# Output gates by tanh, the gates of chunks 1 to 5 on 80 rows, and a new early order

## The chip, the core and the metric

One core of a Trainium2 chip runs the whole program once. The metric is device time in microseconds of one execution; before the change it is 418.37 us (median of 3 runs, 418.22 to 418.58).

## The reference, cut

Three layers follow each other, all in float32: a gated linear attention (an mLSTM) over 2 batches, 8 heads, 768 steps of 40 features, a product of two projections, and a layer with the Mish function.

```python
for t in range(S):                       # attention, per batch and head
    m_new = np.maximum(f_gate[:, :, t] + m, i_gate[:, :, t])
    f_stab = np.exp(f_gate[:, :, t] + m - m_new)
    i_stab = np.exp(i_gate[:, :, t] - m_new)
    C = f_stab * C + i_stab * outer(v_t, k_t);  n = f_stab * n + i_stab * k_t
    o = 1.0 / (1.0 + np.exp(-o_gate[:, :, t]))
    y[:, :, t] = o * (C @ q_t) / np.maximum(np.abs(n @ q_t), 1.0)
h = ((x @ w1) * (x @ w2)) @ w3           # 1536 x 320 -> 1024
x = h @ w_out
h = x @ w_in                             # 320 -> 2048
out = (h * tanh(softplus(h))) @ w_out2
```

## The kernel before, in words

**Tiling.** The 768 steps are 6 chunks of 128; a unit is one chunk of one batch with its 8 heads, so there are 12 units, u = 2 * chunk + batch. Two chunks of both batches are a block of 512 tokens, and the two later layers run block by block (3 blocks). A unit is a chain over the engines: `E` (TensorE, exponents of the decay), `dw` (ScalarE, exp), `vw` (GpSimd, weighted values), `S` (TensorE, q times k), `wg` (VectorE, S times weights), `Y` (TensorE), `I` (TensorE, the state's part), `U` and `st` (state update), `cb` (VectorE, sum of both parts), `r1` to `r3` (denominator), `xs` and `xo` (output gate and denominator), `dup`, `X` (transposes), `Xe` and `Xl` (high and low half of the result for the next layer). The state of one batch passes from unit u to u + 2. `A`, `B` are the products with w1 and w2, `W` is w3 times w_out, `X1` the product with that, `H` and `O` the last layer. Weights come as pieces (load, `mag`, `clamp`, `bits1` to `bits`, `hi`, `lo`): float64 bits turned into two float32r parts, mostly on VectorE.

**Gates.** `start()` prepares the decays. f and i lie on all 128 partitions as 8 copies of the 16 rows (batch, head). Chunk 0 goes first, then the stages chunk 1 and chunks 2 to 5: running maximum `pa` (L879), two tensor_tensor `pt`, `pb` (L895), prefix sum `pc` (L900), then splits into high and low parts `lr`, `ll`, `less`, `la0`, `la1`, `lb0`, `lb1`; `te` transposes the sums on TensorE and `turn` takes their exponent. `rb` and `rc` spread a chunk's sums over the heads (ex_r).

**Order.** Each step is a node with an engine, a due time (table DUE), a duration, and dependencies. `Work.plan` places the nodes by these and so fixes the order of every engine's instructions. Where it sees TensorE idle it puts in products nobody reads, `keep_warm` (L594, tile psz), which keep TensorE's clock up; their number is fixed in the program. Engines wait for each other by semaphores when it runs, each in its own fixed order.

**Output gate.** `add_sigmoids` (L814) applies Sigmoid to 2 and then 4 tiles, on ScalarE; `xs` multiplies by it on GpSimd. The sigmoid needs another function table than exp.

Of the kernel before, what the change touches and what calls it, by code (L numbers as in the profile page):

```python
# [10 lines left out]
F32 = mybir.dt.float32  # L11
# [15 lines left out]
    sgg=(2, 4), mu=8, s_pe=0.268, s_act=0.543, s_dve=0.435, s_pool=0.206, ahead=1, w0n=5, ff=0.972, gd=0.0,  # L27
    ph=0.071, a0=-12.81, ap=-93.853, a_ld=-1652.39, e_e=8363.2, e_s=3345.95, e_r=2252.59, g_ld=6316.58,
# [3 lines left out]
    c_o2=88.35, cp_o2=12.531, c_wi=-5894.32, c_o3=-2264.6, m0=232.0, grp=8, mp0=-162.897, mp=204.465, m_o=1263.83,  # L32
# [3 lines left out]
    mag_w12='ACT', mag_wo='ACT', mag_w3='ACT', mag_wi='DVE', mag_o2='DVE', mag_o3='DVE', lo_w12='DVE', lo_wo='DVE',  # L36
    lo_w3='POOL', lo_wi='POOL', lo_o2='DVE', lo_o3='DVE', xo='POOL', vw='POOL', dup='ACT', rb0='DVE', rc0='DVE',
    rb1='DVE', rc1='DVE', rb='ACT', rc='ACT', st0='DVE', cb0='DVE', prep='ACT', g_tt='DVE', g_ll='DVE',
    lo_w120='DVE', lo_w121='DVE', lo_w122='DVE', lo_w123='DVE', lo_w124='DVE', lo_w125='POOL', lo_w126='DVE',
    lo_w127='POOL',  # L40
# [4 lines left out]
    set_0=0.0, ld_o_0=0.6, ld_g=1.3, ld_qk_0=1.7, ld_kv_0=1.8, load_0=1.9, ld_o_1=4.6, lr_0=4.8, less_0=2.3,  # L45
    ll_0=4.5, la1_0=5.1, la0_0=5.4, rb_0=5.6, one_0=5.7, lb0_0=40.7, lb1_0=6.2, pl_1=6.1, rc_0=6.4, pl_0=18.6,
    E_0=5.8, pa_1=7.7, pr_1=15.4, pa_2=7.8, E_1=7.5, dw_0=8.0, ld_qk_1=8.7, pt_1=9.7, S_0=9.2, pt_2=9.4,
    ld_kv_1=23.2, pb_1=10.6, dw_1=7.0, pb_2=11.3, pc_1=11.4, pc_2=11.7, te_1=16.7, lr_1=11.5, turn_1=7.0,
    less_1=13.1, te_2=11.7, lr_2=24.7, less_2=13.8, load_1=14.8, turn_2=13.5, ll_2=13.9, la1_2=13.7, ll_1=14.5,
    sgm_0=14.3, ld_o_2=24.2, vw_0=4.4, lb1_2=13.6, U_0=-11.7, ld_qk_2=16.0, rb_1=11.7, wg_0=16.2, la0_2=16.4,  # L50
    sgm_1=17.3, vw_1=16.8, ld_kv_2=16.6, la1_1=16.9, st_0=17.9, Y_0=-10.7, la0_1=13.8, mag_0=16.9, lb0_2=18.8,
    lb0_1=19.0, set_1=19.1, lb1_1=-2.1, rc_1=19.4, S_1=19.3, clamp_0=20.0, rb_2=20.1, cb_0=20.6, load_2=18.4,
    E_2=18.1, wg_1=21.0, xs_0=23.9, r1_0=19.4, mag_1=20.5, E_3=22.0, ld_o_3=20.4, r2_0=17.9, bits1_0=11.3,
    dw_2=20.6, U_1=22.5, r3_0=27.8, bits2_0=25.1, Y_1=22.8, ld_qk_3=23.3, st_1=23.8, xo_0=31.7, bits_0=26.7,
    ld_kv_3=26.0, dw_3=23.6, S_2=24.4, cb_1=24.0, vw_2=24.7, r1_1=24.3, I_2=-2.3, rc_2=25.2, wg_2=26.2, U_2=27.2,
    xs_1=31.5, dx_2=25.6, dup_0=23.1, Ie_2=29.8, hi_0=26.6, E_4=28.1, load_3=16.7, st_2=38.2, Y_2=28.6, dw_4=29.5,
# [1290 lines left out]
```

## Time and profile before

| what | value |
|---|---|
| median of 3 runs | 418.37 us |
| the profiled execution, its time | 418.2 us |
| its span | 416.5 us |
| TensorE (PE) busy | 409.5 us, 98% |
| VectorE (DVE) busy | 291.1 us, 70% |
| ScalarE (ACT) busy | 197.7 us, 47% |
| GpSimd (POOL) busy | 80.4 us, 19% |

A row of a timeline gives start, duration, engine, line, operation, output<-inputs, shape and how many were merged. The duration of merged products includes the last one's drain, so the price of a block is the distance from its start to the start of the next one. Times are from the start of the span.

### The profile page before, as it was taken

The numbers are of one execution on the slowest core, as the hardware profiler recorded it, in microseconds if no ns is written. First come the engines' busy times: TensorE is split into PE (matmuls) and PEld (weight loads), VectorE is DVE, ScalarE is ACT, GpSimd is POOL, SyncE is SP. The second block draws the span as 40 slices with busy tenths as digits, with TensorE's granted clock in tenths as the row PEclk, the third lists the DMA queues.
The fourth block names the chain that finished last, engine by engine and source line by source line (L and its number), as shares of the span: only waits on it lengthen the run. The fifth ranks groups of instructions, "written<-read, shape, count | busy, mean of one in ns | idle before, by whom it ended". The sixth has DMA issues, their size and how long they took to land.

```text
span 416.5 us, 7129 instructions
## 1 busy us (share of the span) xinstructions
PE 409.5 (98%) x2815; PEld 359.8 (86%) x2815; DVE 291.1 (70%) x527; ACT 197.7 (47%) x381; POOL 80.4 (19%) x78
## 2 busy tenths in 40 slices
PE   8999999999999999999999999999999999999996
PEld 5689988798888899988888888989989999889995
DVE  7999999999899969779999987789231041330221
ACT  8787967444544444542644376157051161340430
POOL 3234264345102242431001132300000000000000
PEclk9999999999999999999999999999999999999999
DMA  7957744433313543445243253420100000100002
GB/s 238 324 178 220 239 119 153 139 97 127 114 50 102 168 136 101 150 139 166 65 104 87 64 127 90 164 63 2 65 0 2 0 2 2 63 2 0 2 2 64
DMA packets 30497, 40.88 MB, mean 98 GB/s; under 512 B 1856, under 2 KB 24640, under 8 KB 30464
## 3 DMA queue, kind: packets, MB, share of 16 engines
q1 hardware_dynamic: 29952, 39.95, 31.4%
q8 instruction: 22, 0.36, 0.4%
q10 hardware_dynamic: 512, 0.48, 0.4%
q14 instruction: 11, 0.09, 0.1%
HBM read 38.45 MB, written 1.97 MB: 97 GB/s over the span
## 4 chain that ended last, share of the span: by engine, by line
PE 93%; DVE 5%; DMA 1%; ACT 0%; issue 0%; DVEq 0%
PE pso L1210 21%; PE psh L1186 20%; PE psb L1057 11%; PE psa L1057 10%; PE psw L1028 7%; PE psY L699 5%; PE psS L650 3%; PE psx L1097 3%; PE psx L1099 3%; PE psx L1098 3%; PE psI L661 2%; PE psx L1102 1%; PE psx L1101 1%; PE psE L624 1%; DVE gates L410 1%; PE psX L743 1%
## 5 line engine op out<-in xcount | busy, mean ns | idle before, releaser
L410 DVE TENSOR_TENSOR gl<-u,gh 128x512 fp32r<-128x512 f32 x48 | 32.9, 691 | 68.7 <-ACT u L1195 68.7
L1191 ACT ACTIVATE gh<-psh 128x512 fp32r<-128x512 f32 x48 | 28.8, 601 | 79.5 <-PE psh L1186 79.4
L1186 PE MATMUL psh<-xd,wih 64*128 64x512 f32 x240 | 59.4, 395 | 0.0
L1186 PEld LDWEIGHTS psh<-xd,wih 64*128 64x128 f32 x240 | 43.1, 184 | 3.6 <-ACT u L1195 0.2
L1210 PE MATMUL pso<-wo,gh 128*128 128x320 f32 x192 | 42.6, 310 | 0.0
L1186 PE MATMUL psh<-hs,wih 64*128 64x512 f32 x144 | 41.6, 395 | 0.0
L502 DVE SCALAR_TENSOR_TENSOR f<-raw,f 128x640 int32<-128x640 int32 (+2 forms) x44 | 40.0, 908 | 0.9
L507 DVE SCALAR_TENSOR_TENSOR f<-raw,f 128x640 int32<-128x640 int32 (+2 forms) x44 | 37.7, 858 | 0.9
L410 POOL TENSOR_TENSOR th<-f,th 128x512 fp32r<-128x512 f32 x16 | 22.1, 1381 | 62.1 <-ACT th L512 59.1
L1210 PEld LDWEIGHTS pso<-wo,gh 128*128 128x128 f32 x192 | 32.0, 188 | 1.1 <-issue 1.1
L1186 PE MATMUL psh<-xd,wil 64*128 64x512 f32 x120 | 31.6, 391 | 0.0
L1186 PE MATMUL psh<-hs,wil 64*128 64x512 f32 x120 | 31.4, 391 | 0.0
L1210 PE MATMUL pso<-wo2h,gh 128*128 128x320 f32 x96 | 30.0, 312 | 0.0
L1210 PE MATMUL pso<-wo2h,gl 128*128 128x320 f32 x96 | 29.6, 309 | 0.0
L1210 PE MATMUL pso<-wo2l,gh 128*128 128x320 f32 x96 | 29.6, 309 | 0.0
L1210 PE MATMUL pso<-wo,gl 128*128 128x320 f32 x96 | 29.6, 309 | 0.0
L1057 PE MATMUL psa<-hs,w12h 128*128 128x512 f32 x72 | 28.9, 401 | 0.1
L1195 ACT ACTIVATE u<-psh 128x512 f32<-128x512 f32 x48 | 28.9, 603 | 0.0
L1057 PE MATMUL psb<-hs,w12h 128*128 128x512 f32 x72 | 28.3, 394 | 0.2 <-DVE y L410 0.2
L1186 PEld LDWEIGHTS psh<-hs,wih 64*128 64x128 f32 x144 | 25.7, 184 | 3.2 <-issue 1.3
L1028 PE MATMUL psw<-woh,th 128*128 128x320 f32 x128 | 28.5, 310 | 0.0
L493 DVE TENSOR_SCALAR f<-f 128x640 f32<-128x640 f32 (+2 forms) x44 | 23.6, 536 | 7.0 <-ACT f L487 6.3
(146 smaller groups left out, 1031.8 us busy)
## 6 DMA issues: line engine op xcount, KB each, us to landing
raw<-in_w_dram SPq DMA_DIRECT2D x16, 512.0 KB
raw<-in_w_out_dram SPq DMA_DIRECT2D x12, 640.0 KB
raw<-in_w_dram SPq DMA_DIRECT2D x16, 384.0 KB
raw<-in_w_in_dram SPq DMA_DIRECT2D x16, 320.0 KB
kv<-in_kv_dram SPq DMA_DIRECT2D x12, 324.0 KB
qk<-in_qk_dram SPq DMA_DIRECT2D x24, 160.0 KB
sg<-in_o_gate_dram SPq DMA_DIRECT2D x12, 160.0 KB
out_dram<-yo SPq DMA_DIRECT2D x9, 160.0 KB
```

The source lines that it names most:

```text
L410: return eng.tensor_tensor(out=o, in0=a, in1=b, op=op)
L493: nc.vector.tensor_scalar(out=ff, in0=ff, scalar1=HI_MIN, scalar2=HI_MAX, op0=ALU.max, op1=ALU.min)
L502: nc.vector.scalar_tensor_tensor(out=f, in0=t["raw"][:, :, 1], scalar=-0x40000000, in1=f, op0=ALU.bitwise_and, op1=ALU.bitwise_or)
L507: nc.vector.scalar_tensor_tensor(out=f, in0=t["raw"][:, :, 0], scalar=29, in1=f, op0=ALU.logical_shift_right, op1=ALU.bitwise_or)
L650: nc.tensor.matmul(t["S"][g][:, p * T:(p + 1) * T], lhsT=t["qk"][rows, 1, p, :], rhs=t["qk"][rows, 0, p, :], start=True, stop=True)
L699: nc.tensor.matmul(ps[:, h * VW:(h + 1) * VW], lhsT=t["w"][:, h, :], rhs=t["v"][:, h, :], start=True, stop=True)
L1028: nc.tensor.matmul(ps, lhsT=t[a][:, 0, c * 128:(c + 1) * 128], rhs=wo[b], start=(c0 + c + s == 0), stop=(c0 + c == KC - 1 and s == 2))
L1057: nc.tensor.matmul(ps, lhsT=a, rhs=b, start=(n == 0 and not begun), stop=(n == len(seq) - 1))
L1186: nc.tensor.matmul(mt[i + k]["ps"], lhsT=w[k][:, c], rhs=x[k][c], start=(n == 0 and c == 0), stop=(n == 2 and c == KC2 - 1))
L1191: nc.scalar.activation(out=t["gh"], in_=t["ps"], func=AF.Mish)
L1195: nc.scalar.activation(out=t["u"], in_=t["ps"], func=AF.Mish)
L1210: nc.tensor.matmul(ps, lhsT=t[a][:, sl], rhs=wo[b], start=(ft == 0 and n == 0), stop=(ft == KF2 - 1 and n == 2))
```

## The change

1. The output gates use Tanh at half the argument, so that sigmoid is (tanh + 1) / 2; `xs` becomes one scalar_tensor_tensor (plus 1, times y) on VectorE, and `r2` doubles the denominator. One gate tile per instruction, 6 times.
2. The gates of chunks 1 to 5 are computed on 80 rows (5 chunks x 16) of 128 columns: one running maximum of 16 rows x 640 (`pa`), five products that put the maxima on the 80 rows (`mv`), one pass of `pt`, `pc`, `less`, a split (`lr`, `ll`, `la`, `lb`), ten products that spread them back over 128 partitions (`rp`), and nine copies out of PSUM (`evL`, `ev0`, `ev1`). `prep_sel` builds the selection matrices on GpSimd. The gate loads shrink from 2 x 128 x 640 to 2 x 16 x 640 plus 2 x 80 x 128.
3. The decay of the state, `sd`, is a node of its own, on GpSimd for units 2, 3, 5, 6, 7 and 9, on VectorE for 4 and 8.
4. The causal mask by TensorE is for 7 units instead of 8 (`mu`); unit 7 gets it from GpSimd (`ms`).
5. New due times for the first hundred microseconds, `keep_warm` at the start 7 instead of 5, rules that prefer the same form of product, and a guard that adds `keep_warm` products. The last layer may use more buffers in the last block.

```diff
-    sgg=(2, 4), mu=8, ... ahead=1, w0n=5, ff=0.972, gd=0.0,
+    sgg=(1, 1, 1, 1, 1, 1), mu=7, ... ahead=1, w0n=7, ff=1.0,
+    gd=0.316, ph=1.362, ...
...
-    la0_0=5.4, ...
+    ... sd_8=67.5, sd_6=75.5, evL_0=15.3, rp_1=-0.1, ps_0=35.2, ...
...
-            if c > 0:
-                s = st[b].rearrange("a p (e v) -> a (p e) v", e=2)
-                tt(nc.vector, s, s, t["d"].unsqueeze(2).to_broadcast([128, H, VW]), mult)
+        def sd():
+            s = st[b].rearrange("a p (e v) -> a (p e) v", e=2)
+            tt(nc.gpsimd if sd_e == "POOL" else nc.vector, s, s, t["d"].unsqueeze(2).to_broadcast([128, H, VW]), mult)
...
-            nc.vector.tensor_scalar_max(out=t["r"], in0=t["r"], scalar1=1.0)
+            (nc.gpsimd if r2_e == "POOL" else nc.vector).tensor_scalar(out=t["r"], in0=t["r"], scalar1=1.0, scalar2=2.0,
+                                                                        op0=ALU.max, op1=mult)
...
-            tt(nc.gpsimd if ENG["xo"] == "POOL" else nc.vector, xh, t["y"][:, :, 0:D], sg[kb, b][:, j % 2], mult)
+            nc.vector.scalar_tensor_tensor(out=xh, in0=sg[kb, b][:, j % 2], scalar=1.0, in1=t["y"][:, :, 0:D], op0=add, op1=mult)
...
-                nc.scalar.activation(out=o, in_=o, func=AF.Sigmoid)
+                nc.scalar.activation(out=o, in_=o, func=AF.Tanh, scale=0.5)
...
+        def ld_c():
+            for o, a in ((f1, f_gate), (i1, i_gate)):
+                nc.sync.dma_start(out=o, in_=a[0:G, F:S])
+            for o, a in ((cf, f_gate), (ci, i_gate)):
+                nc.sync.dma_start(out=o, in_=by_chunk(a[0:G, F:S]))
+        def mv():
+            gps["m"] = bank("psg")
+            for c in range(NK):
+                a = F + c * T
+                nc.tensor.matmul(gps["m"][0:NC, 0:T], lhsT=sel_m[:, NC - G - c * G:2 * NC - G - c * G], rhs=m[0:G, a:a + T],
+                                 start=(c == 0), stop=(c == NK - 1))
+        def rp(n):
...
+                for e in range(2):
+                    a = 32 + c % 2 * G - 32 * e
+                    nc.tensor.matmul(o, lhsT=sel_r[r, a:a + 128], rhs=chi[r, 2 * e * T:2 * (e + 1) * T], start=(e == 0), stop=(e == 1))
+        add_node(("pa", 1), "DVE", due, scan(S1), lambda: nc.vector.tensor_tensor_scan(
+            out=m[0:G, F + 1:S + 1], data0=f1, data1=i1, initial=m[0:G, F:F + 1], op0=add, op1=ALU.max), [("ld_c",)], port=True)
+        add_node(("mv", 1), "PE", due, 1.1, mv, [("pa", 1), ("ps", 0)], [(AT, [("pt", 1)])], warm=0.3)
```

**ScalarE, the first microseconds.** Names: ex_l and ex_r are the operands of `E`, sel_b and sel_h constants for them; CAST gates 64x128 is `lr` of chunk 0. Before:

```order
L871 CAST causal<-z 128x512
L857 CAST ex_l_88<-sel_b 64x128
L857 CAST ex_l_89<-sel_b 64x128
L905 CAST gates<-gates 64x128
L931 ACTIVATE ex_l_89<-gates,neg_b 64x128
L931 ACTIVATE ex_l_88<-gates,neg_b 64x128
L867 ACTIVATE ones_92<-ident 64x128
```

and with the change:

```order
L919 CAST causal<-z 128x512
L895 CAST ex_l_88<-sel_b 64x128
L895 CAST ex_l_89<-sel_b 64x128
L895 CAST ex_l_88<-sel_b 64x640
L895 CAST ex_l_89<-sel_b 64x640
L1032 CAST gates<-gates 64x128
L905 ACTIVATE ones_92<-ident 64x128
L905 ACTIVATE ones_93<-ident 64x128
L1016 ACTIVATE ex_l_88<-gates,neg_b 64x128
```

The two copies of 640 columns now stand ahead of `lr` of chunk 0; before they came after it.

**VectorE, from `ll` of chunk 0 to the first `wg`** (w<-psS). Before:

```order
L410 TENSOR_TENSOR gates<-gates 32x128
L410 TENSOR_TENSOR ex_r_90<-gates,sel_h 64x512
L935 SCALAR_TENSOR_TENSOR ex_l_89<-gates,neg_b,ex_l_89 32x128
...
L879 SCALAR_TENSOR_TENSOR gates<-gates 128x512
L410 TENSOR_TENSOR gates<-gates 128x512 x2
L410 TENSOR_TENSOR gates<-gates 128x128 x2
...
L900 SCALAR_TENSOR_TENSOR gates<-gates 128x128 x5
...
L935 SCALAR_TENSOR_TENSOR ex_l_89<-gates,neg_b,ex_l_89 32x512
L410 TENSOR_TENSOR w<-psS,w 128x4x128 x2
```

and with the change:

```order
L418 TENSOR_TENSOR gates<-gates 32x128
L1047 SCALAR_TENSOR_TENSOR gates<-gates 16x640
L1019 SCALAR_TENSOR_TENSOR ex_l_89<-gates,neg_b,ex_l_89 32x128
L418 TENSOR_TENSOR ex_r_90<-gates,sel_h 64x512
...
L418 TENSOR_TENSOR gates<-gates,psg 80x128
L418 TENSOR_TENSOR gates<-gates 80x128
L935 TENSOR_SCALAR gates<-gates 80x128
L936 SCALAR_TENSOR_TENSOR gates<-gates 80x128
L940 SCALAR_TENSOR_TENSOR gates<-gates 80x128
L418 TENSOR_TENSOR split<-gates,split 80x128
L418 TENSOR_TENSOR w<-psS,w 128x4x128 x2
```

The running maximum of all later chunks moved ahead of the operands of the first `E`, and six short instructions take the place of the long ones.

**TensorE, from the first products to the second `Y`.** psz is `keep_warm`, psg the gates (`mv`, `te`, `rp`). Before, from the end of the first four `E` pairs:

```order
L650 MATMUL psS<-qk_78 128x128 x8
L594 MATMUL psz<-causal,identr 128x512 x5
L675 MATMUL psU<-vw,kv 40x41 x8
L594 MATMUL psz<-causal,identr 128x512 x2
L943 MATMUL psg<-ident,gates 128x16
...
L943 MATMUL psg<-ident,gates 128x16 x4
L594 MATMUL psz<-causal,identr 128x512 x10
L699 MATMUL psY<-kv,w 128x41 x8
L623 MATMUL psE<-causal,identr 128x512
```

and with the change, from the same place, which now has `te` (psg<-ident) between the `E` of unit 0 and that of unit 1:

```order
L1024 MATMUL psg<-ident,gates 128x80
...
L663 MATMUL psS<-qk_78 128x128 x8
L688 MATMUL psU<-vw,kv 40x41 x8
L606 MATMUL psz<-causal,identr 128x512 x4
L715 MATMUL psY<-kv,w 128x41 x8
L975 MATMUL psg<-split,sel 128x256 x10
L663 MATMUL psS<-qk_79 128x128 x8
L688 MATMUL psU<-vw,kv 40x41 x8
L606 MATMUL psz<-causal,identr 128x512 x6
L715 MATMUL psY<-kv,w 128x41 x8
L606 MATMUL psz<-causal,identr 128x512 x2
L674 MATMUL psI<-st_80,qk_78 128x82 x4
```

The `E` of units 2 and 3, which came right after the first `Y` and ahead of the second, now come after both; `keep_warm` products are 21, 1, 4, 6 and 2 up to there, against 12, 5, 2, 2 and 10.

## Rows read from the trace of the kernel before

**Rows 1.** Busy time by stretch: us, busy us and count of each engine, granted clock, DMA.

```profile
0.00:10.00 10.00, 8.14 (x22) 5.57 (x24) 7.84 (x21) 8.12 (x16) 3.88 (x14) 1.00 0.77 231
...
350.00:400.00 50.00, 50.00 (x387) 45.46 (x386) 12.17 (x19) 16.25 (x32) 0.00 (x0) 1.00 0.04 14
```

**Rows 2.** The keep_warm line: count, duration ns min/median/max, first and last start.

```profile
L594 PE MATMUL psz<-causal,identr x33: 388/396/796, 4.4 to 36.8; 128*128 128x512 f32 x33
```

**Rows 3.** Timeline of TensorE, first products: start us, us, what.

```profile
4.37 3.35 PE L594 MATMUL psz<-causal,identr 128*128 128x512 f32 x7 [0.35 <-ACT causal L871]
...
15.53 2.56 PE L594 MATMUL psz<-causal,identr 128*128 128x512 f32 x10 [0.31 <-ACT eT L947]
17.94 2.18 PE L699 MATMUL psY<-kv,w 128*128 128x41 f32 x16
```

**Rows 4.** Timeline of TensorE, 25 to 38 us.

```profile
25.59 1.10 PE L661 MATMUL psI<-st,qk 128*128 128x82 f32 x8
...
26.66 1.16 PE L650 MATMUL psS<-qk 40*128 40x128 f32 x16
27.76 0.51 PE L675 MATMUL psU<-vw,kv 128*40 128x41 f32 x16
28.19 0.98 PE L594 MATMUL psz<-causal,identr 128*128 128x512 f32 x3
29.01 0.39 PE L623 MATMUL psE<-causal,identr 128*128 128x512 f32 x1
...
29.94 1.87 PE L699 MATMUL psY<-kv,w 128*128 128x41 f32 x16
31.64 0.48 PE L623 MATMUL psE<-causal,identr 128*128 128x512 f32 x1
...
36.00 1.17 PE L594 MATMUL psz<-causal,identr 128*128 128x512 f32 x4
37.01 1.88 PE L699 MATMUL psY<-kv,w 128*128 128x41 f32 x16
```

**Rows 5.** Timeline of VectorE, 5 to 18 us: gates and the first wg.

```profile
5.35 0.29 DVE L410 TENSOR_TENSOR gates<-gates 32x128 fp32r<-32x128 f32 x1
5.67 0.69 DVE L410 TENSOR_TENSOR ex_r<-gates,sel_h 64x512 fp32r<-64x512 f32 x1
6.37 0.34 DVE L935 SCALAR_TENSOR_TENSOR ex_l<-gates,neg_b,ex_l 32x128 fp32r<-32x128 f32 x1
...
7.87 1.81 DVE L879 TENSOR_TENSOR_SCAN gates<-gates 128x128 f32<-128x128 f32 x2
9.71 2.50 DVE L410 TENSOR_TENSOR gates<-gates 128x512 f32<-128x512 f32 x4
...
17.02 1.29 DVE L410 TENSOR_TENSOR w<-psS,w 128x512 f32<-128x512 f32 x2
```

**Rows 6.** Timeline of VectorE, 18 to 26 us: work between the first and second wg.

```profile
18.22 0.66 DVE L692 COPY st<-psU 40x164 f32<-40x164 f32 x2
...
22.13 0.50 DVE L711 COPY y<-psY 128x328 f32<-128x328 f32 x1
...
23.94 0.55 DVE L493 TENSOR_SCALAR f<-f 128x768 f32<-128x768 f32 x1
...
25.69 0.96 DVE L502 SCALAR_TENSOR_TENSOR f<-raw,f 128x768 int32<-128x768 int32 x1
```

**Rows 7.** Timeline of ScalarE, 5 to 18 us.

```profile
5.02 0.29 ACT L905 CAST gates<-gates 64x128 fp32r<-64x128 f32 x1 [0.19 <-DVE gates L900]
...
6.44 0.72 ACT L857 CAST ex_l<-sel_b 64x640 fp32r<-64x640 f32 x1
...
16.40 1.28 ACT L814 ACT_TABLE_LOAD   x1
```

**Rows 8.** Groups by form, 0 to 110 us (VectorE) and the whole span (GpSimd).

```profile
L410 DVE TENSOR_TENSOR st<-st,d 128x328 f32<-128x328 f32 x8 | 4.4, 548 | 0.3 <-ACT d L639 0.3
...
L410 POOL TENSOR_TENSOR vw<-kv,w 128x328 f32<-128x328 f32 x10 | 9.9, 992 | 20.4 <-DMA kv<-in_kv_dram 17.8 <-DMA qk<-in_qk_dram 2.6
```

More of the change, by code (lines that the diff above doesn't have):

```diff
@@ L322, in plan @@
             if e == "PE" and self.form[n] != form:
[L323 removed]
+                last += TUNE["sw"]
                 form = self.form[n]
@@ L330, in plan @@
                 port = free[e]
-            if size:
+            if size < 0:
+                end[n] = free[e] - size
+            if size > 0:
                 dma = max(dma, s + 1.6) + max(0.45, size / 243e3)
@@ new lines, in gate_sum, with less, cut @@
+        def gate_sum(f, i, L, skip=0):
+            nc.vector.tensor_scalar(out=f, in0=i, scalar1=0.0, scalar2=-120.0, op0=ALU.min, op1=ALU.max)
+            nc.vector.tensor_tensor_scan(out=L[:, skip:], data0=one[0:L.shape[0], skip:], data1=f[:, skip:], initial=0.0,
+                                         op0=mult, op1=add)
+        def less(i, L):
+            nc.vector.scalar_tensor_tensor(out=i, in0=i, scalar=0.0, in1=L, op0=ALU.max, op1=add)
+        def cut(a, c):
+            return a[:, c * T:(c + 1) * T]
@@ new lines, in start @@
+        for b in range(B):
+            add_node((f"la{b}", 0), "ACT", due, act(T) + 0.1, lambda b=b: la(b), [("less", 0)])
+            add_node((f"lb{b}", 0), "DVE", due, dve(T), lambda b=b: lb(b), [(f"la{b}", 0)], port=True)
+        due = K["g1"]
+        for b in range(B):
+            add_node(("pl", b), ENG["prep"], due - 2, act(640) if ENG["prep"] == "ACT" else 0.75,
+                     lambda b=b: prep_l(b, T, S, ENG["prep"]))
+        add_node(("pr", 1), ENG["prep"], due - 1, act(1024) if ENG["prep"] == "ACT" else 1.2,
+                 lambda: prep_r(1, ENG["prep"]))
@@ new lines, in start @@
+        add_node(("pc", 1), "DVE", due, dve2(T) + scan(T), lambda: gate_sum(cf, ci, cL), [("pt", 1)], port=True)
+        add_node(("less", 1), "DVE", due + 1, dve(T), lambda: less(ci, cL), [("pc", 1)], port=True)
+        for k, (nm, nl, a, x) in enumerate((("lr", "ll", cL, "pc"), ("la", "lb", ci, "less"))):
+            h, l = chi[:, k * T:(k + 1) * T], chi[:, (2 + k) * T:(3 + k) * T]
+            add_node((nm, 1), "ACT", due, act(T), lambda h=h, a=a: nc.scalar.copy(h, a), [(x, 1)])
+            add_node((nl, 1), "DVE", due, dve(T), lambda h=h, l=l, a=a: tt(nc.vector, l, a, h.bitcast(F32), sub), [(nm, 1)], port=True)
@@ L1154, with group @@
     MH = places("b", 4)
-    GP, UP, YP = places("z", 16), places("z", 4, 16), places("z", 6, 25)
+    UP = places("z", 4, 16)
+    def group(i):
+        return next((a, b) for a, b in zip(K["grp"], K["grp"][1:]) if a <= i < b)
     acc = {}
```

407 lines of the change are left out of this document (220 added, 187 removed).

## The prediction

> **What bounds the kernel now.** I read the busy times by stretch first. In the last stretch TensorE is busy 50.00 of 50.00 us while VectorE has 45.46 [rows 1]; in the first ten microseconds it is busy 8.14 us at a mean granted clock of 0.77. So late on only the amount of TensorE's work counts, and at the start a chain over other engines does. Over the whole run TensorE is busy 98% of the span. Some of that is filler: the keep_warm line has 33 rows [rows 2], the first at 4.4 and the last at 36.8 us. So the question for any saving on VectorE, ScalarE or GpSimd is whether it lets TensorE begin its real work earlier, and the question for any saving on TensorE is how many real products go.
>
> Then I read TensorE's timeline. The first seven fillers take 3.35 us, nearly half a microsecond each, which is the lower clock level; the ten from 15.53 to the start of Y at 17.94 take 2.41 us, 0.24 each, the upper one [rows 3]. Before 17.94 TensorE waits for the gates. From there on it is packed, but for two fillings: three keep_warm products from 28.19 to 29.01 (0.82 us) and four from 36.00 to 37.01 (1.01 us) [rows 4]. Prices are taken from one start to the next in the same rows: I 1.07, S 1.10, U 0.43, E of a unit 0.93, Y 1.70.
>
> What the packed part waits for at its start is VectorE's chain. After the three operands of unit 0 (0.69, 0.34 and their like) come the scans of the later chunks (1.81 us from 7.87), four 128x512 passes (2.50 us) and the rest of the gates, until the first wg at 17.02 [rows 5]: 9.15 us in which no wg could run. That is the place where the change could earn something.
>
> **The change part by part.** The comparison is made at one point, the start of S of unit 2, since by then both orders have done the same products: E of units 0 to 3, S, U and Y of 0 and 1, I of 2. Before, that is at 26.66 us [rows 4].
>
> *The start.* ScalarE's copy of unit 0's gate now stands behind two 640-column copies of 0.72 us each; it ran at 5.02 for 0.29 us [rows 7], and I put it at about 6.1 to 6.4. VectorE's ll then ends near 6.75. The one scan of 16x640 has as many columns as the two scans that took 1.81 us [rows 5], with one start less: 1.6 us, to 8.35. Unit 0's four operands (two of 0.34, two of 0.69, and gaps) go to 10.45. Before, all that was over at 7.87, so unit 0's E is some 2.6 us later. E ends about 10.9. Four instructions on 80x128 follow; the nearest rows are the 0.29 and 0.34 of 32x128 [rows 5], and with gaps they take 1.45 us, to 11.9. If they cost as much as the widest of the short ones, 0.55 for 128x768 [rows 6], that would be 0.9 more; below, I allow a tenth off the whole chain. The transpose of the sums waits for them, and TensorE with it, about 1.0 us. Then E of unit 1 from 12.1, S of unit 0 until 14.2, wg of unit 0 from 14.4 to 15.7 (1.29 [rows 5]). This wg started at 17.02 before: the shorter gates win 2.6 us here, though the operands came later. Y of unit 0 would end at 17.4, where before it started at 17.94 and ended 1.70 later, near 19.65.
>
> *Between the first and second wg.* The ten spreading products have half a filler's columns, so half its 0.24: 1.2 us together. S and U of unit 1 follow, to 20.2, then six fillers (1.45), to 21.6. VectorE has meanwhile st 0.66, the second xs in its new form about 0.50 (the 128x328 copy is the nearest row), cb 0.50 and one 128x768 bits pass 0.96 [rows 6]; two state decays of 0.55, from the eight that took 4.4 us [rows 8]; one operand of 0.69 [rows 5]; small and PSUM copies of 0.29 and 0.42 (between 0.29 for 128 and 0.69 for 512 columns). Their sum is 5.6; I take 5.4, as one of them may slip behind. So the second wg runs from 21.1 to 22.4, and TensorE has waited 0.8 us. Y of unit 1 to 24.1, two fillers 0.5, I 1.07, E of units 2 and 3 1.9: S of unit 2 starts at 27.6. **The term is +0.95 us.** The 2.3 us by which the first Y ended earlier are spent on the ten products, more fillers, and a second wg that is not brought forward as much as the first.
>
> For the lower end: with no wait from 11.9 on, te 0.2, the products and fillers named sum to 14.6, and S of unit 2 starts at 26.7, the term is nil. For the upper end, the short instructions at 0.55: +1.85.
>
> *After that.* Both orders have seven more fillers. In before they took 0.82 + 1.01 = 1.83 us [rows 4]; in the change they stand as 1, 1, 2, 2 and 1, 7 x 0.24 = 1.7. **-0.15 us.** They are written into the program and take their time whether a wait is there or not.
>
> *The causal mask* for seven units instead of eight takes away two products of the filler's shape, 2 x 0.24 [rows 3]: **-0.48 us**, since TensorE is packed there. GpSimd does it instead, in about 1.5 us.
>
> *Tanh.* It shares a table with the exponent, so the order has two loads left of six, 4 x 1.28 us [rows 7] less on ScalarE. I cost it at nothing: ScalarE is busy 47% of the span, and in the packed part TensorE waits for it only where the fillers stand, which stay. The xs on VectorE adds about 12 x 0.5, what the gates save there is about as much, and six state decays of 0.55 leave [rows 8]. Nothing on TensorE's path is late by it before the last block, and there 4.5 us of 50 are free [rows 1].
>
> *The gate loads* shrink by 0.49 MB, 2 us at the 231 GB/s of the first stretch [rows 1]. I book nothing, because the first chain waits for unit 0's gate and ScalarE, not for these; kv comes earlier by it, which helps GpSimd.
>
> *The sum.* 0.95 - 0.15 - 0.48 = +0.3 us on the profiled execution of 418.2 us: 418.5. The median lies 0.17 above that execution, so **418.7 us** against 418.37. A measurement can tell some 0.2% here, 0.84 us; this is no measurable change, with bounds of the early term from 417.75 to 419.6.
>
> **The rivals.** *The early chain is shorter than booked (faster).* The chain on VectorE runs from 6.75 to 22.4. If the 80-row instructions and the PSUM copies cost a tenth less in all (1.5 us of 15.7), TensorE's waits of 1.0 and 0.8 us mostly go, and the time is 1.4 less: 417.3. For it: half of that chain has only one nearest row, and fewer partitions move less. Against it: a 64x512 operand at 0.69 us is no quicker per column than the 128x512 passes, 2.50 for four [rows 5], so rows don't matter, columns do, and those I have counted.
>
> *The state decay on GpSimd stands in a queue (slower).* The decay took 0.55 us on VectorE and would take 0.99 on GpSimd by the vw of the same shape; those ten vw have 20.4 us of idle time ahead of them, 17.8 of it for kv by DMA [rows 8]. GpSimd works in its order: a decay placed behind a vw whose kv hasn't landed waits for that load, and the state, I and Y of unit u + 2 behind it. For unit 5 the order has it behind the vw of units 4 and 5. If kv lands 1.6 us after the decay is ready, its extra 0.44 and this make 2.0 us in a packed TensorE: 420.7. It decides from the point where kv of unit 5 lands after the decay's exponent. Against it: the 17.8 us are a sum of ten, mostly GpSimd early at a load, and the gate loads leave DMA freer.
>
> *The clock (slower).* The two fresh gaps near 11 and 21.6 us could drop the granted clock to its lower level. Before, TensorE also waited ahead of 15.53, and the ten fillers behind ran at 0.24 us [rows 3], the upper level, so a gap of that size cost nothing. If it does here, E, S and U behind the gap (2.46 us) run at half rate, and with what follows that is +2.0: 420.7. The Trainium skill ("TensorE: Matmul & The Clock Gate", "HAM oscillation — how this bites in real kernels") says that idle gaps between bursts throttle the engine again and each next burst starts cold, which speaks against an order that waits ahead of te; by it the sum would be 420.7. The trace so far goes the other way.
>
> *Tanh brings table loads of its own (slower).* Then ScalarE has some six loads more than the order shows, two of them at 1.28 us ahead of an exponent that is waited for: 421.3. The order has one load ahead of the Mish table, so I hold this unlikely.
>
> **How the numbers follow.** The forecast has 0.46, of which 0.06 lies above +0.2%, by the upper bound of the early term. The shorter chain has 0.31, the queue 0.14, the clock 0.06, the tables 0.03. So faster 0.31, same 0.40, slower 0.29. The forecast's own range is 417.8 to 419.6. The whole one goes down to 416.8, half a microsecond beyond the shorter chain's time, leaving out perhaps a third of that case (0.10), and up to 421.0, which takes in the queue and the clock with some left over (0.08 out).
>
> **What would show it.** In the changed profile's TensorE timeline: unit 0's E done near 10.9 us, a gap of about 1.0 ahead of te, the first Y from 15.7, the second from 22.4, S of unit 2 at 27.6, 0.95 later than before. If S of unit 2 starts at 26.7 or earlier, the shorter chain was right; if it is at 27.6 and the end is over 420, the loss lies later: then look at I of unit 7 with a wait for GpSimd's decay. Granted clock under 1.00 past 10 us would show the clock. Table loads on ScalarE should be two. The forecast is wrong if from 28 us to the end TensorE's idle time or its products' total differ by more than half a microsecond from the -0.6 booked, or if a wait of another kind, for the transposes or for xs on VectorE, stands in the list of waits.

## The result and the profile after

The changed kernel took 422.12 us in the median of 22 runs (418.46 to 433.91), beside 418.38 us for the kernel before in the same sessions. The ratio, over the runs that lie within 1.5% of each kernel's fastest, is 1.0061 (1.0043 to 1.0079), or about 420.9 us: slower. The range (416.8 to 421.0) holds that by 0.1 us, though the median of all runs lies outside it; the likeliest case, no measurable change, is not what happened.

The runs of the changed kernel lie in groups, and each group has its granted clock: 418.5 to 419.4 us at 0.996 to 1.000, 420.3 to 420.7 at 0.994, 422.1 to 423.2 at 0.988 to 0.992, and one of 433.91 at 0.962. So there are two questions, what the kernel takes at full clock, and why it so seldom has it. A mean of 0.996 can hide a fall to half the clock for some 3 us, as a profile below shows (`mask8`), so the table counts all runs below 0.998. With the runs of the experiments' sessions:

| kernel | runs | median, us | lowest | median at a clock of 0.998 or more (runs) | runs below 0.998 (at 0.995 or less) |
|---|---|---|---|---|---|
| before | 84 | 418.44 | 418.03 | 418.38 (65) | 19 (6) |
| changed | 34 | 422.02 | 418.46 | 419.04 (9) | 25 (21) |

The 22 runs of the kernel before in the session of the result have no clock on record and are not in the table; three of them took 426.4 to 426.8 us. So the kernel before loses its clock too, but in fewer of its runs. In what follows, full clock means a mean of 0.998 or more.

The profiled execution of the changed kernel is one of full clock: 419.22 us, span 417.5 us. Its busy times from 20 to 25 us (stretch, us, then busy us and count for PE, PEld, DVE, ACT, POOL, then granted clock, DMA share, GB/s):

```profile
20.00:25.00 5.00, 4.26 (x30) 3.49 (x28) 4.71 (x10) 4.92 (x14) 0.51 (x2) 1.00 0.95 281
```

and the same stretch of the kernel before, in which TensorE is busy throughout:

```profile
20.00:25.00 5.00, 5.00 (x53) 3.91 (x51) 4.58 (x10) 4.18 (x8) 0.82 (x1) 1.00 0.76 240
```

A correction first. The prediction read 0.77 in [rows 1] as the granted clock. It is the DMA share; the clock is the column before it, 1.00. And yet the first fillers take nearly twice as long as later ones [rows 3]: the granted clock doesn't show TensorE's slow first microseconds, the products' spacing does.

TensorE's timeline of the changed kernel, from the transpose of the sums to S of unit 2, and two places later on (start us, us, what, and in brackets the idle time ahead of it and its end):

```profile
11.73 0.29 PE L1024 MATMUL psg<-ident,gates 80*128 80x80 f32 x1 [0.25 <-DVE gates L936]
...
15.50 1.87 PE L715 MATMUL psY<-kv,w 128*128 128x41 f32 x16
17.31 0.75 PE L975 MATMUL psg<-split,sel 32*128 32x256 f32 x10
17.98 1.16 PE L663 MATMUL psS<-qk 40*128 40x128 f32 x16
...
19.51 1.66 PE L606 MATMUL psz<-causal,identr 128*128 128x512 f32 x6
21.72 0.42 PE L715 MATMUL psY<-kv,w 128*128 128x41 f32 x2 [0.56 <-DVE w L418]
22.32 1.75 PE L715 MATMUL psY<-kv,w 128*128 128x41 f32 x14 [0.18 <-DVE w L418]
23.91 0.71 PE L606 MATMUL psz<-causal,identr 128*128 128x512 f32 x2
24.45 1.01 PE L674 MATMUL psI<-st,qk 128*128 128x82 f32 x8
...
27.41 0.83 PE L663 MATMUL psS<-qk 40*128 40x128 f32 x10
...
40.50 1.09 PE L674 MATMUL psI<-st,qk 128*128 128x82 f32 x8 [0.16 <-issue]
...
48.27 0.53 PE L674 MATMUL psI<-st,qk 128*128 128x82 f32 x3 [0.29 <-DMA qk<-in_qk_dram]
```

The first Y is at 15.50 instead of 17.94, S of unit 2 at 27.41 instead of 26.66 [rows 3, 4]: +0.75, where +0.95 was forecast. What the prediction called VectorE's chain reads as follows:

```profile
6.64 1.54 DVE L1047 TENSOR_TENSOR_SCAN gates<-gates 16x640 f32<-16x640 f32 x1
...
14.19 1.29 DVE L418 TENSOR_TENSOR w<-psS,w 128x512 f32<-128x512 f32 x2 [1.02 <-PE psS L663]
...
18.41 0.95 DVE L514 SCALAR_TENSOR_TENSOR f<-raw,f 128x768 int32<-128x768 int32 x1
19.28 0.47 DVE L999 TENSOR_SCALAR ex_l<-psg,neg_b 64x256 fp32r<-64x256 f32 x1
19.84 0.69 DVE L418 TENSOR_TENSOR ex_r<-gates,sel_h 64x512 fp32r<-64x512 f32 x1
20.73 0.34 DVE L999 TENSOR_SCALAR ex_l<-psg,neg_b 64x128 fp32r<-64x128 f32 x1 [0.20 <-ACT gates L991]
21.00 1.27 DVE L418 TENSOR_TENSOR w<-psS,w 128x512 f32<-128x512 f32 x2
```

The scan took 1.54 us (forecast 1.6), the first wg came at 14.19 (14.4), the second at 21.00 (21.1). Between them VectorE is nearly full, so the second wg starts when the steps ahead of it, the last four shown, are done.

### The profile page after: what moved, and what is told of

It reads as the page before. It is cut to its first block, busy times and chain, and to the rows that moved or that the text cites. A ratio compares the mean times of both kernels' runs of the same rounds, so it can differ in the third digit from the quotient of the medians.

```text
span 417.5 us, 7175 instructions
## 1 busy us (share of the span) xinstructions
PE 410.6 (98%) x2832; PEld 359.8 (86%) x2832; DVE 280.5 (67%) x521; ACT 192.5 (46%) x379; POOL 73.2 (18%) x80
## 4 chain that ended last, share of the span: by engine, by line
PE 92%; DVE 3%; ACT 2%; DMA 2%; issue 1%; SPq 0%; ACTq 0%; DVEq 0%
PE pso L1302 20%; PE psh L1278 20%; PE psb L1144 11%; PE psa L1144 11%; PE psw L1115 7%; PE psY L715 4%; PE psx L1184 3%; PE psx L1185 3%; PE psx L1186 3%; PE psS L663 2%; PE psI L674 2%; DMA qk<-in_qk_dram 2%; PE psx L1189 1%; PE psx L1188 1%; PE psE L636 1%; PE psX L762 1%
## 5 line engine op out<-in xcount | busy, mean ns | idle before, releaser
L418 DVE TENSOR_TENSOR gl<-u,gh 128x512 fp32r<-128x512 f32 x42 | 29.0, 692 | 66.2 <-ACT u L1287 66.2
L1283 ACT ACTIVATE gh<-psh 128x512 fp32r<-128x512 f32 x42 | 25.2, 600 | 80.6 <-PE psh L1278 80.6
L519 DVE SCALAR_TENSOR_TENSOR f<-raw,f 128x640 int32<-128x640 int32 (+2 forms) x44 | 36.6, 834 | 0.4
L514 DVE SCALAR_TENSOR_TENSOR f<-raw,f 128x640 int32<-128x640 int32 (+2 forms) x44 | 36.0, 821 | 0.5
L418 POOL TENSOR_TENSOR th<-f,th 128x512 fp32r<-128x512 f32 x16 | 21.0, 1318 | 62.9 <-ACT th L524 52.2
L505 DVE TENSOR_SCALAR f<-f 128x640 f32<-128x640 f32 (+2 forms) x44 | 21.6, 496 | 7.9 <-ACT f L499 7.7
L499 ACT ACTIVATE f<-raw 128x512 f32<-128x512 f32 (+2 forms) x28 | 21.3, 759 | 11.7 <-POOL th L418 7.6
L1278 PE MATMUL psh<-ls,wih 64*128 64x512 f32 x96 | 26.3, 390 | 0.0
L418 POOL TENSOR_TENSOR wil<-f,wih 128x640 fp32r<-128x640 f32 x8 | 15.8, 1994 | 59.6 <-ACT wih L524 59.6
```

The source lines that it names most:

```text
L418: return eng.tensor_tensor(out=o, in0=a, in1=b, op=op)
L499: nc.scalar.activation(out=t["f"].bitcast(F32), in_=t["raw"][:, :, 1].bitcast(F32), func=AF.Abs)
L505: nc.vector.tensor_scalar(out=ff, in0=ff, scalar1=HI_MIN, scalar2=HI_MAX, op0=ALU.max, op1=ALU.min)
L514: nc.vector.scalar_tensor_tensor(out=f, in0=t["raw"][:, :, 1], scalar=-0x40000000, in1=f, op0=ALU.bitwise_and, op1=ALU.bitwise_or)
L519: nc.vector.scalar_tensor_tensor(out=f, in0=t["raw"][:, :, 0], scalar=29, in1=f, op0=ALU.logical_shift_right, op1=ALU.bitwise_or)
L1278: nc.tensor.matmul(mt[i + k]["ps"], lhsT=w[k][:, c], rhs=x[k][c], start=(n == 0 and c == 0), stop=(n == 2 and c == KC2 - 1))
```

## Experiments

All run in the order that the planner gave to the changed kernel (or to the one before), with single entries of that order edited. An entry that is a number is a batch of `keep_warm` products; the batches are counted from 0. So each edit is a few numbers: `fills` gives a batch another count, and a step is taken out of the order and put behind another. The edits are shown shortened, with the old counts as comments.

### The changed kernel once more

No edit.

> The changed kernel unchanged. Its 22 times lie in groups: about 419.2 us at a mean granted clock of 0.996 to 1.000, about 420.5 at 0.994 and 422.1 to 423.2 at 0.988 to 0.992. Theory A (the clock): in the longer executions TensorE runs part of the first 30 us at its lower level; a profile of such a one shows a stretch of granted clock clearly under 1.00 and products of 0.4 us and more in it, all else equal, and 3 us more at the start of S of unit 2. Theory B (a wait): a longer execution has a TensorE gap behind a transfer that lands late, with products of 0.24 us around it. If this profile is of the short group, it only has to repeat 419.2 and S of unit 2 at 27.4.

421.09 us in the median of 12 runs; six at 0.996 to 1.000 (418.53 to 420.24) and six at 0.992 and less. The profiled one was the longest, 435.29 us at 0.961, and so shows the fall of the clock large. Its stretches:

```profile
20.00:24.00 4.00, 2.90 (x17) 2.17 (x17) 3.73 (x9) 3.52 (x9) 0.25 (x1) 1.00 0.99 289
24.00:31.00 7.00, 7.00 (x27) 6.07 (x26) 4.98 (x9) 3.53 (x11) 1.10 (x2) 0.52 0.61 219
31.00:43.00 12.00, 12.00 (x129) 10.42 (x127) 9.34 (x23) 8.39 (x22) 4.65 (x7) 0.99 0.43 122
43.00:72.00 29.00, 28.70 (x169) 24.93 (x169) 17.04 (x38) 14.67 (x38) 10.28 (x12) 0.53 0.48 142
72.00:100.00 28.00, 27.88 (x248) 23.72 (x248) 24.04 (x45) 13.64 (x28) 7.29 (x7) 1.00 0.45 141
```

And its TensorE around the first fall:

```profile
19.93 1.66 PE L612 MATMUL psz<-causal,identr 128*128 128x512 f32 x6
22.51 0.42 PE L721 MATMUL psY<-kv,w 128*128 128x41 f32 x2 [0.92 <-DVE w L424]
23.11 2.12 PE L721 MATMUL psY<-kv,w 128*128 128x41 f32 x14 [0.18 <-DVE w L424]
25.03 1.20 PE L612 MATMUL psz<-causal,identr 128*128 128x512 f32 x2
26.03 1.83 PE L680 MATMUL psI<-st,qk 128*128 128x82 f32 x8
```

From 20 to 24 us TensorE was busy 2.90 us of 4. Then, from 24.3, the clock is at its lower level, half, until 31 us: the second Y's tail, the two fillers at 0.5 us each, I in 1.83 instead of 1.01, E of units 2 and 3. S of unit 2 starts at 31.36, 3.95 later than in the profile of full clock. At 44.8 it falls again and stays down until the wide products with w1 and w2 have begun (72.1). In between TensorE is the slow one (28.70 us busy of 29 with the clock at half). Theory A holds for this execution; TensorE waits for no transfer here. The wait ahead of the second Y (0.92 and 0.18 us for 0.56 and 0.18) grew because the fourteen early fillers took 4.41 us instead of 3.78 and because a VectorE step of 0.56 us took 0.98.

### Filling the wait at 21 us

```diff
+        fills = {3: 9}     # six before
```

> Nine instead of six products that nobody reads ahead of the second Y, where TensorE waits 0.74 us for the weights of unit 1; nothing else moves. Theory A with the wait at 21 us as its place: the longer executions go, all times near 419.2 to 419.4 (three products are 0.72 us and fit into the wait). Theory A with another place (the start, or ahead of te): as many longer executions as in the changed kernel, about half or more of them. Theory B: as many too.

Median 420.77 us, six of 12 runs at 0.994 and less (the other six 418.82 to 420.96). In its profile, of full clock, the second Y starts at 21.70, so there the three cost nothing; the four runs of full clock have 419.59, against 419.04. The longer executions do not go: three more products in the wait are not enough. Where they fall is not known, since no fallen execution of this kernel was profiled; and a wait of 1.4 us, as in the next kernel's profile, is longer than three products, so this run doesn't clear the wait.

### The mask of unit 7 back on TensorE

```diff
-                if pe_mask:
+                if pe_mask or u == 7:
                     nc.tensor.matmul(t["E"][e], lhsT=identr, rhs=causal, start=True, stop=False)
```

> The two mask products of unit 7 are put back on TensorE, with the order of all else kept, GpSimd's masking too. Theory: they lie in the packed part, so in executions of like clock +0.48 us against the changed kernel (419.2 to 419.7). Rival: TensorE has slack there (a wait behind them shrinks by as much), so no change.

At full clock: 419.33 us (5 runs) against 419.04, +0.29 by the medians and +0.61 by the means, with 0.48 expected. The sign is right, and the runs size it no better than that. Five of 12 runs are at 0.994 and less. The profiled one has 422.50 us and a mean clock of 0.996, and yet its clock is 0.50 from 25 to 28 us. The edit changes nothing before unit 7, so its early part is one more execution of the changed kernel. What came ahead of the fall (ScalarE, VectorE, TensorE):

```profile
15.11 0.74 ACT L843 ACTIVATE sg<-sg 128x640 f32<-128x640 f32 x1 [1.48 <-DMA sg<-in_o_gate_dram]
16.99 0.56 DVE L511 TENSOR_SCALAR f<-f 128x768 f32<-128x768 f32 x1 [0.51 <-ACT f L505]
22.38 0.42 PE L721 MATMUL psY<-kv,w 128*128 128x41 f32 x2 [1.23 <-DVE w L424]
```

and ScalarE in the kernel before, where the first gate tiles follow behind `eT`, from 16.40 [rows 7]:

```profile
15.26 0.22 ACT L947 ACTIVATE eT<-psg 128x64 f32<-128x64 f32 x1
```

The tanh of the second gate tile waits 1.48 us for its load (0.49 in the profile of the result). Behind it in ScalarE's fixed order stand `eT`, a split and the step of the weights (`f`) that VectorE waits for; the second wg is at 21.65 instead of 21.00, and TensorE waits 1.41 us at the second Y instead of 0.74. So theories A and B are not rivals here: a load that lands late makes the wait longer, and the clock falls behind the wait.

### Function tables

```diff
-                nc.scalar.activation(out=o, in_=o, func=AF.Tanh, scale=0.5)
+                nc.scalar.activation(out=o, in_=o, func=AF.Sigmoid, scale=0.5)
```

> The six gate activations use the sigmoid function in place of tanh, the order kept; the output gates get a wrong value, the work is the same but for twelve function table loads of 1.28 us on ScalarE. Theory of the prediction: ScalarE's loads are covered while TensorE is packed, so what four loads saved was nothing: twelve give at most 1 us in executions of like clock, through the three gate tiles before 20 us. Rival: ScalarE's exponents are waited for, and each pair of loads ahead of one costs up to 2.6 us on TensorE: 3 us or more in all.

425.68 us, and all six runs at 0.992 and less. Four of them, at 0.991 and 0.992, have a median of 425.0, beside 422.3 for eleven runs of the changed kernel at the same clocks: +2.7 us for twelve loads, and a fall of the clock in every run. ScalarE and TensorE of the profiled one:

```profile
14.15 1.28 ACT L843 ACT_TABLE_LOAD   x1
15.44 0.74 ACT L843 ACTIVATE sg<-sg 128x640 f32<-128x640 f32 x1
16.18 1.28 ACT L1033 ACT_TABLE_LOAD   x1
17.61 0.28 ACT L1061 CAST split<-gates 80x128 fp32r<-80x128 f32 x1
```

```profile
17.95 1.07 PE L981 MATMUL psg<-split,sel 32*128 32x256 f32 x10 [0.59 <-ACT split L1061]
```

Two loads stand ahead of the split that the spreading products wait for. So the loads are not free here, and the "at most 1 us" expected was for covers that this order doesn't have. The run doesn't price the four loads that the kernel before had more, since those stood at other places.

### More fillers around the second Y

```diff
+        fills = {3: 9, 4: 6}     # six and two before
```

> Seven more products that nobody reads around the second Y: nine instead of six ahead of it, six instead of two behind it. In the disturbed profile of the changed kernel the granted clock fell behind the wait ahead of the second Y (6 products and a wait of over a microsecond, then 2.5 us of narrow products), at about 24 us. Theory A (the fall comes of how little TensorE does from 19.5 to 25 us): it no longer falls there, nearly all executions have a clock of 0.996 or more; three fit into the wait and four cost 0.24 each, so about 420.0 in nearly all, and a median below the changed kernel's 421 to 422. Rival (the fall comes of what went before, at the start): as many executions at 0.994 and less as before, median 422 or more.

Five of six runs at 0.998 to 1.000 (419.74 to 420.48), one at 0.996 (422.93); median 420.16. Seven products more cost 1.04 us at full clock (420.08 against 419.04). Its stretches where the other profile fell:

```profile
20.00:25.00 5.00, 4.82 (x29) 3.96 (x29) 4.72 (x10) 4.91 (x14) 0.52 (x2) 1.00 0.93 282
25.00:30.00 5.00, 5.00 (x43) 3.99 (x43) 3.59 (x7) 3.00 (x8) 1.81 (x2) 1.00 0.79 262
```

One of six is below 0.998, where the changed kernel has 25 of 34, `fill21` 8 of 12 and `zstart`, run in the same session, 5 of 10. That speaks for theory A, that it matters what TensorE has to do in this stretch. Six runs are few, four more products behind the second Y were not tried without the three ahead of it, and the last experiments show that it isn't the only such place.

### Fewer fillers at the start

```diff
+        fills = {0: 10}     # fourteen before
```

> Ten instead of fourteen of the second batch of early fillers, so that the products that spread the maxima (which waited behind the fillers in the disturbed profile, 9.43 instead of 8.81 us) are not held up by them. Theory A: the clock falls at 24 us all the same, so as many low executions as in the changed kernel; undisturbed ones at 418.7 to 419.2, since there the products behind the fillers were not waited for. Rival (late start of these products makes the wait at 21 us longer, and that brings the fall): fewer low executions. Third: fewer products at the start let the clock rise later, E of unit 0 at half rate, and more low executions.

419.70 us at full clock (5 runs) and five of ten at 0.994 and less. Still many falls, as theory A had it: these four fillers are not what brings them. That the full-clock runs are some 0.6 us slower was expected by none; in the profile the second gate tile waits 0.96 us for its load and the second Y is at 21.88, 0.16 later.

### Taking fillers out of the kernel before

```diff
+        fills = {4: 2}     # ten before
```

> The kernel before with two instead of ten fillers ahead of its first Y, where TensorE waits for the weights anyway; nothing on the path goes. Theory A (it is TensorE's thin stretches that bring the lower clock): the kernel before now shows what the changed one shows, a granted clock of 0.994 and less in half or more of its executions and 420 to 423 us in these; the others stay at 418.4. Rival (the clock has nothing to do with fillers): times and clocks as before, 418.4 in nearly all.

427.76 us, 422.75 to 440.82, all six runs at 0.942 to 0.987. Its stretches and the place of the fall:

```profile
15.00:20.00 5.00, 2.69 (x12) 2.10 (x11) 4.79 (x10) 4.90 (x10) 0.74 (x1) 0.79 1.04 320
20.00:25.00 5.00, 5.00 (x25) 4.16 (x27) 2.59 (x5) 3.94 (x8) 0.81 (x1) 0.50 0.59 195
```

```profile
15.38 0.73 PE L600 MATMUL psz<-causal,identr 128*128 128x512 f32 x2 [0.32 <-ACT eT L953]
18.11 3.81 PE L705 MATMUL psY<-kv,w 128*128 128x41 f32 x16 [1.99 <-DVE w L416]
```

The first Y starts at 18.11 as ever (17.94 with ten), so the fillers were not on the path. Without them its sixteen products take 3.6 us instead of 2.0, and the E and S behind it take longer as well. This is the plainest of the runs: all six fall, while none of the 20 runs of the kernel before in that session is below 0.996. The kernel before keeps its clock in this place by these products.

### The mask of unit 7 by GpSimd in the kernel before

```diff
-                if pe_mask:
+                if pe_mask and u != 7:
                     nc.tensor.matmul(t["E"][e], lhsT=identr, rhs=causal, start=True, stop=False)
...
+            if u == 7:
+                ms()
```

> The kernel before with the mask of unit 7 by GpSimd instead of TensorE, all else in its order: part 4 of the change alone. Prediction: two products of 0.24 us less in the packed part, -0.48 us, 417.9, with the clocks of the kernel before. Rival: the weights of unit 7 come later by GpSimd's 1.5 us and its S or Y waits, so no gain or up to +1 us.

No gain. At full clock 419.04 us (4 runs) against 418.38, +0.66, and seven of 11 runs at 0.995 and less, median 420.41. VectorE and then GpSimd in its profile, where the mask now is:

```profile
48.66 1.09 DVE L727 TENSOR_SCALAR r<-r 128x8 f32<-128x8 f32 x1
```

```profile
48.52 1.21 POOL L642 TENSOR_SCALAR_AFFINE_SELECT w<-w 128x1016 f32<-128x1016 f32 x1 [1.96 <-ACT w L635]
```

and VectorE in the kernel before:

```profile
48.90 0.16 DVE L719 TENSOR_SCALAR r<-r 128x8 f32<-128x8 f32 x1
```

An instruction of 0.16 us lasts 1.09, as long as GpSimd's mask goes on, and what follows on VectorE is about a microsecond later (the next wg at 53.47 instead of 52.33). The Trainium skill ("SBUF — State Buffer", "Terms") says that VectorE and GpSimd arbitrate for one pair of ports and the loser waits for the whole instruction; the two rows agree with it. How much of the 0.66 this stall makes was not tested. It is a matter of the order: in the changed kernel's profile GpSimd's mask of unit 7 (51.01, 1.13 us) runs beside no VectorE instruction that it stretches. Then the clock (first this kernel's stretches, then those of the kernel before):

```profile
51.00:53.00 2.00, 1.78 (x15) 1.62 (x15) 1.95 (x7) 2.00 (x4) 0.74 (x1) 0.59 0.92 337
53.00:58.00 5.00, 5.00 (x15) 3.81 (x14) 3.30 (x7) 1.05 (x4) 1.58 (x2) 0.50 0.00 2
```

```profile
51.00:53.00 2.00, 2.00 (x21) 1.70 (x20) 1.92 (x6) 2.00 (x4) 1.07 (x2) 1.00 0.75 251
53.00:58.00 5.00, 5.00 (x58) 4.14 (x56) 4.44 (x8) 3.86 (x7) 2.21 (x3) 1.00 0.02 3
```

It fell at 51 us, and from 45 to 51 TensorE was busy 5.88 us of 6, with S, X and Y and the two E products that were left. The two mask products that were taken away were wide ones in a stretch of narrow ones. Whether their absence or the short waits brought the fall, this run does not tell apart.

### Two moves that shorten the early chain

The last four kernels take the sum's own reading of the early chain at its word. `w_first` puts three VectorE steps behind the second wg; `lr_first` puts ScalarE's two wide copies behind lr and la; `both` has both moves, `both_z` four fillers more.

```diff
+        W = [(("bits2", 0), ("rc", 1)), (("ev0", 2), ("rc", 1)), (("rb", 1), ("st", 1))]
+        L = [(("pl", 0), ("la1", 0)), (("pl", 1), ("pl", 0))]
+        w_first:  moves W,     fills = {3: 2}
+        lr_first: moves L,     fills = {0: 8}
+        both:     moves W + L, fills = {0: 8, 3: 2}
+        both_z:   moves W + L, fills = {0: 8, 3: 3, 4: 5}
```

> The changed kernel with three VectorE steps that stand ahead of the second wg put behind it and the state update (a bits pass of 0.95 us, a copy from PSUM of 0.34 that waits, an operand of 0.69), and two instead of six fillers ahead of the second Y. Theory of the sum: the second wg sets when the second Y runs, so wg starts at 19.3 instead of 21.0, Y of unit 1 at 20.0 instead of 21.7, S of unit 2 at 25.8 instead of 27.4, and in executions of full clock 417.5. Rival: E of unit 2 then waits for its two operands on VectorE and the gain is given back there, 418.5 or more. On the clock: if it falls because of the wait ahead of the second Y, it falls less often than in the changed kernel; if it falls because the products of this stretch are narrow, wait or no wait, it falls as often or more, 420 to 423 in these.

> The changed kernel with the two 640-column copies on ScalarE behind lr and la of unit 0 instead of ahead of them, and eight instead of fourteen of the second early fillers. Theory of the prediction's first term: lr was 1 us late by them and VectorE's whole chain to the first and second wg with it; VectorE's idle 1.08 us ahead of ll goes to 0.1, the first Y starts at 14.5 instead of 15.5, S of unit 2 at 26.4, and 418.1 in executions of full clock. Rival: the running maximum waits for its load, or the products behind it for the fillers, so nothing is won by 15 us; 419.1.

> Both moves. By the sum the two add: S of unit 2 at 24.8, 416.5 in executions of full clock, which is below both kernels. Rival: VectorE, with the late steps piled behind the second wg, is now late for wg of unit 2, and half of it comes back, 417.8. The clock as for the single moves: fewer thin microseconds, but also fewer fillers (six and four less).

> Both moves, with four fillers more than that around the second Y (three ahead, five behind). Theory A: that keeps the clock at 0.996 or more in nearly all executions, for 4 x 0.24 us more: 417.5 in nearly all, below the kernel before by its median too. Rival: the clock falls at another thin place, 43 to 53 us, as often as in the changed kernel; then the median stays above 419.

| kernel | second Y, S of unit 2 in the profile, us | lowest | at 0.998 or more (runs) | at 0.995 or less | median |
|---|---|---|---|---|---|
| changed | 21.72, 27.41 | 418.46 | 419.04 (9) | 21 of 34 | 422.02 |
| w_first | 20.09, 26.08 | 417.89 | 418.56 (4) | 8 of 13 | 420.24 |
| lr_first | 23.74, 33.81 (clock fell at 24) | 418.54 | 418.69 (2) | 8 of 12 | 422.52 |
| both | 19.74, 26.28 | 417.86 | 417.87 (2) | 10 of 12 | 420.11 |
| both_z | 19.59, 25.98 | 417.42 | 417.49 (3) | 9 of 12 | 421.99 |

`w_first` did at the second Y what the sum said (20.09 for 20.0, S of unit 2 at 26.08 for 25.8), but of the 1.33 us there 0.5 is left at the end, at full clock; where the rest went its profile, of a fallen clock, doesn't show. `lr_first` brought the first Y to 14.64, but in its profile the second Y is at 23.74, two microseconds later than in the changed kernel, behind a gate load as in `mask8`:

```profile
15.91 0.74 ACT L845 ACTIVATE sg<-sg 128x640 f32<-128x640 f32 x1 [3.13 <-DMA sg<-in_o_gate_dram]
23.74 0.44 PE L723 MATMUL psY<-kv,w 128*128 128x41 f32 x2 [2.51 <-DVE w L426]
```

Two runs of full clock are too few to price it. With both, S of unit 2 is not at 24.8 but at 26.28. The next wait has come up, and it is neither rival's:

```profile
19.74 0.41 PE L723 MATMUL psY<-kv,w 128*128 128x41 f32 x2 [0.21 <-DVE w L426]
...
23.24 1.09 PE L682 MATMUL psI<-st,qk 128*128 128x82 f32 x8 [0.60 <-DMA qk<-in_qk_dram]
```

I of unit 2 waits for its own q and k, which no one moved. At full clock `both` (2 runs) and `both_z` (3) are under the kernel before by 0.5 and 0.9 us, and their lowest (417.42) under its lowest (418.03). By the median of all runs neither is: ten and nine of their 12 runs are at 0.995 or less. In the profiles of `w_first` and `both_z` it fell not at 24 us but near 40, each time around a wait ahead of I of unit 5:

```profile
40.35 1.98 PE L682 MATMUL psI<-st,qk 128*128 128x82 f32 x8 [0.96 <-DVE y L426]
```

```profile
40.03 1.15 PE L682 MATMUL psI<-st,qk 128*128 128x82 f32 x8 [1.13 <-DMA qk<-in_qk_dram]
```

So none of these kernels is ahead of the kernel before both at full clock and in the median of all runs. Of the versions of the changed one `both`, `zmid`, `zstart` and `w_first` have the best medians, 420.11 to 420.24, and are not told apart.

The ten profiles of the changed kernel and of its versions with tanh fall in two groups at the second Y. TensorE's idle time there is 1.10, 1.41 and 2.67 us in `again`, `mask8` and `lr_first`, whose clock fell at 24 to 25 us, and 0.18 to 0.89 us in the seven whose clock stayed up at that place. This is how the profiles lie; the late loads came by themselves, and no run brings one about.

## Why the prediction was right and wrong

**The early term, +0.95.** Right in size and in what sets it: +0.75 measured, with lr, the scan, both wg and the first Y within 0.3 us of where they were put. Several prices inside it were off. The ten spreading products took 0.68 us instead of 1.2, and the gap ahead of the transpose was 0.25 instead of 1.0, mostly because E of unit 0 itself ran later. The second Y began at 21.72, not 22.4, since its first two products start before the wg ends. None of this moved S of unit 2, because the second wg sets the end of that Y. And the second wg was right by luck in part: the two state decays counted ahead of it on VectorE are not there (the first stands at 39.70), two 128x768 passes of 0.55 and 0.56 us are, at nearly the same price, and the prices named add up to 5.1, not 5.6, with one copy of each size.

**The shorter chain, 0.31.** It did not happen: S of unit 2 is at 27.41, not at 26.7 or earlier.

**The fillers after that, -0.15.** Wrong by 0.5: seven took 2.18 us, +0.35 against 1.83. They stand in five batches, and a batch of one costs 0.31 to 0.34 us, one of two 0.57 to 0.64; 0.24 was the price within a long batch.

**The mask, -0.48.** Right for the products: those of E from S of unit 2 on sum to 6.32 us, 6.79 before. As a term of the time it depends on the order around it. Put back in the changed kernel, they cost 0.29 to 0.61, which fits; taken from the kernel before, their removal costs 0.66, where GpSimd's mask holds up VectorE. That GpSimd "does it instead" was booked at nothing.

**What is left from S of unit 2 to the end** is +0.27 at full clock, where -0.63 was booked. By the forecast's own sign, half a microsecond, it is wrong here. Besides the fillers, the transposes X took 0.46 more and S 0.58 more from their starts to the next one's, I 0.36 less; the waits ahead of I of units 5 and 6 (0.16 and 0.29 us in the rows above) lie in the first two, and the rest is not traced to a cause. At full clock the whole comes to +0.66 (419.04 against 418.38), inside the forecast's own range of 417.8 to 419.6.

**Tanh at nothing.** Not settled. The profile has two table loads on ScalarE, as forecast, so the rival of more loads did not happen. The loads can stand on the path (`sigm`), so a saving at the right place could be worth something; the four that went were not tried in the kernel before. What was overlooked is where the tanh now stands: its wait for the gate load comes ahead of steps that the second wg needs, and this load lands late in some executions (`mask8`, `lr_first`).

**The clock rival, 0.06.** This is the step that failed. It named the mechanism and one place, the gap near 21.6 us, and in three profiles the clock fell right behind that gap. It was given 0.06, where 25 of 34 runs are below 0.998 and 21 at 0.995 or less. Its price of 2.0 us was too small for most of them: 3.3 us lie between the medians of the fallen runs (422.37) and of full clock. That its 420.7 is near the 420.9 of the result is luck, since 420.9 averages over fallen runs and others. The argument against it was that the kernel before waits ahead of 15.53 and its ten fillers still run at 0.24 us. They are the reason, as `b_nofill` shows: those ten are what kept the clock. The Trainium skill ("TensorE: Matmul & The Clock Gate", "HAM oscillation — how this bites in real kernels"), by which idle gaps between bursts throttle the engine again, was the better guide; the trace of `b_nofill` agrees, with an idle 1.99 us and then a granted clock of 0.50. What the runs leave open is how much the gap counts and how much the products around it. Three more products in the gap did not do it (`fill21`), seven on both sides did in five of six runs (`zmid`). Narrow products in a row, with hardly a gap, may be a part of it, which `b_mask7` suggests and doesn't prove.

**The queue on GpSimd.** It did not happen: in the profile after no state decay waits for a load, and TensorE is busy 50.00 us of the 50 from 50 to 100 us.

## What to carry to other kernels

Ahead of a reordering, ask of every stretch of narrow products or waits what keeps TensorE's clock up there, and count fillers and wide products that move away as part of the price: here a fall costs some 3 us (422.37 in the median of the runs at 0.995 or less, 419.04 at full clock). Ask also which loads stand ahead of the step that such a stretch waits for, since one that lands late in some executions makes the wait longer in these. Look at the spread and the granted clock of many runs before believing one profile: the profiled execution here, 419.22 us, shows a loss of a fifth of a per cent and no trace of the larger one. And a step moved to GpSimd can still hold up VectorE: look at what runs beside it.

## What was not expected of the hardware

- The first fillers take 0.45 us apiece (seven between 4.37 and 7.52 in the kernel before) at a granted clock shown as 1.00, later ones 0.24.
- The clock, once down at 44.8 us, stayed down for 27 us in one run (`again`) with TensorE busy nearly all the time, until the wide products of A and B.
- GpSimd's mask of 128x1016 stretched a VectorE instruction on 128x8 from 0.16 to 1.09 us.
- A single filler between products of other forms costs 0.31 to 0.34 us, not 0.24.
- A load issued in the same order landed late enough to hold up ScalarE for 0.49 us in one execution and for 1.48 in another.
